# Six lots of query scores instead of four in the main bursts of an attention and cosine-FFN kernel

## The chip, the cores and the metric

One Trainium2 (trn2) chip, one core of it. The metric is device time in microseconds (us); less is better. The time before is 1098.57 us, the median of three runs (1098.48 to 1100.44).

## The reference, cut to what matters

```python
B, N, C = 4, 12480, 128            # 49 agents, float32
scale = 1.0 / np.sqrt(C)
def sm(a, b):                      # softmax of scale * a @ b.T
    s = scale * (a @ b.transpose(0, 2, 1))
    e = np.exp(s - s.max(-1, keepdims=True))
    return e / (e.sum(-1, keepdims=True) + 1e-09)
agent_v = sm(agents, k) @ v        # (4, 49, 128): keys and values of a batch give 49 rows
out = sm(q, agents) @ agent_v      # (4, 12480, 128): every query looks at 49 agents
h = out.reshape(-1, 128) @ w_in    # (49920, 2048)
result = (h * np.cos(h)) @ w_out   # (49920, 128)
```

## The kernel before

The agents' values are multiplied into the first weights, batch by batch, so that the weights of 49 agents for a query (`pT`) go straight into the FFN. The 49,920 queries are 52 groups of 960 (13 for each batch), each in two chunks of 480 columns, and the 2048 hidden units are 8 pairs of 128. **A step** is one pair for one chunk: 16 steps a group, 208 a batch, 832 in all. In step n PE multiplies into `ph` (L1063, two matmuls of 480 columns in one of three `ph` tiles), ScalarE takes the cosine (L1066), VectorE the product `(c - 1) * h` (L1072), and PE multiplies the product of four steps before into the output's accumulator (L1088). At a chunk's end two small matmuls (L1084, L1085) are added and ScalarE copies the accumulator out. That stream goes on from start to end, and everything else is worked into it.

**Lots.** For each group of queries, its scores with the agents must be ready before its first step: 64 small matmuls of 49 columns (`query_parts`, L169), a copy out of PSUM (L689), the maximum over the agents on VectorE (L693), a subtraction on GpSimd (L695), later an exponential, a sum, and the turning into `pT` (L785 to L796: PE, ScalarE, GpSimd). `query_both` does the scores of two groups in one `ph` tile, with one copy (L734) and one maximum (L736). A lot of keys of the next batch is alike, 64 small matmuls, a copy and a running maximum. A lot of values (`values`, L595) is 64 small matmuls with the exponentials of the keys (L516), whose result VectorE copies into `av` (L604, the first) or adds to it (L606). A small lot's result, and the output's accumulator too, is a tile `one`, of which there are two. A lot's queries are loaded from HBM by SP into `xt` (three tiles), its values into `vt` (six).

**When.** `plan` and `early_plan` hold what is to be emitted in which step; `early_plan` comes ahead of the products that are still owed, `plan` behind them. `extra` looks for the next free step whose place in the chunk allows a lot. `spread_out` and `mixed` spread the lots over the steps evenly. A load may not be issued before the loads that were emitted 24 steps earlier. SP issues its loads one after another, each when its tile is free.

**Bursts.** ScalarE's exponentials need another table than its cosine. So they are gathered: in step 97 of every batch's 208 (steps 97, 305, 513, the main bursts, and 721, the last) ScalarE does the exponential of seven groups of queries (L746), of all keys of the next batch (L587) and of six more groups, with a table load before and after (in the last, of five groups alone). For seven steps from there the order on PE, VectorE and ScalarE is the program's (`as_traced`), and the products of the burst's next steps are emitted only with the third step behind it. Here `fill` gives work to the other engines: one lot of queries at the burst's step, two at once (`query_both`) a step later, then one more lot and the first two lots of values, which need the key exponential. `judged` emits four reductions (L381) a step behind the burst and a small verdict (L393, L394) three steps behind it: they look at the folded weights of the batch before and serve a fallback. They are there in the bursts at 305, 513 and 721. The other eleven lots of values, and the lots of queries left of the first seven of the next batch (five in the last batch), are spread over the steps from the burst's + 5 on.

Of the kernel before, what the change touches and what calls it, by code (L numbers as in the profile page):

```python
# [9 lines left out]
F32 = mybir.dt.float32  # L10
# [8 lines left out]
P = 128  # L19
# [22 lines left out]
VT = 6  # L42
# [4 lines left out]
def agent_attention_cos_ffn(ctx, tc, qT, kT, v, vk, vk_rest, agT, w_in, w_out, outT):  # L47
    nc = tc.nc
    NB, _, N = qT.shape
# [5 lines left out]
    DFF = w_in.shape[0] * 512  # L55
# [83 lines left out]
    def load(dst, src):  # L139

        ins = nc.sync.dma_start(dst, src)
        traced = nc.cur_bb.bb.instructions[-1]
        if pinned[0]:
            tc.keep_in_program_order(ins)
        elif len(issued) > AHEAD:
            tc.add_manual_dep(traced, issued[-AHEAD].name, mybir.DependencyInfo(mybir.DependencyClass.NoSync,
                              mybir.DependencyReason.DATA), reason="held")
        latest[0] = traced
# [107 lines left out]
    class Agents:  # L256
# [58 lines left out]
        def value_tile(self, g):  # L315
            vt = self.sb.tile([TT, GT, P], F32, name="vt", bufs=VT)
            for h in range(2):
                load(vt[:, h * HT:(h + 1) * HT], v[self.b, g, h])
            return vt

        def values(self, g):
            vt = self.value_tile(g)
            po = self.psum()[:KR, :P]
            e = self.part(g).rearrange("p t a -> p (t a)")
            for t in range(HT):
                for h, width in enumerate((HI, NA)):
                    x = h * HT + t
                    mm = nc.tensor.matmul(po[h * HI:h * HI + width], e[:, x * NA:x * NA + width], vt[:, x, :],
                                          start=(t == 0), stop=(t == HT - 1))
                    if t == h == 0:  # L330
                        behind(mm)
            if g == 0:
                self.sums = self.sb.tile([KR, P], F32, name="sums", bufs=1)
                nc.vector.tensor_copy(self.sums, po)
            else:
                nc.vector.tensor_add(self.sums, self.sums, po)
# [198 lines left out]
    class Later(First):  # L535
# [53 lines left out]
        def add(self, g):  # L589
            s = self.s[:, 8 * g:min(8 * g + 8, NT_K)]  # L590
            es = self.es[:, :s.shape[1]]
            with kept_behind([nc.gpsimd.engine]):
                nc.gpsimd.tensor_add(es, self.s[:, :8] if g == 1 else es, s)

        def values(self, g):  # L595
            e = self.part(g)
            w, k, _ = e.shape
            vt = self.sb.tile([P, 2 * 4, P], F32, name="vt", bufs=VT)[:w, :k]
            load(vt, vk[self.b, g] if g + 1 < NL else vk_rest[self.b])
            po = self.psum()[:, :NA]  # L600
            self.weighted(po, [e[:, t] for t in range(k)], vt, True, True)
            if g == 0:
                self.clear()
                nc.vector.tensor_copy(self.av[:, :NA], po)  # L604
            else:
                nc.vector.tensor_add(self.av[:, :NA], self.av[:, :NA], po)  # L606
# [28 lines left out]
    with ExitStack() as pools:  # L635
# [40 lines left out]
        def query_parts(n, piece, wide=False, by_vector=False):  # L676
            b, g = n // NG, n % NG
            src = qT[b, :, g * GRP:(g + 1) * GRP]
            if wide:
                ps = scores_twice(sb.tile([P, 2 * 512], F32, name="xt", bufs=3)[:, :GRP], src, b, pair())  # L680
                yield
            else:
                ps = query_scores(sb, src, b, small()).rearrange("p (h t) a -> p h t a", h=2)
                yield
            if n == piece[0]:
                piece_tiles(piece)
            e = e_of[n].rearrange("p (h t) a -> p h t a", h=2)
            if not wide:
                (nc.vector.tensor_copy if by_vector else nc.scalar.copy)(e, ps)  # L689
                ps = e  # L690
            mx = sb.tile([QT, GT], F32, name="mx2")
            mx = mx.rearrange("p (h t) -> p h t", h=2)
            nc.vector.reduce_max(mx, ps, axis=AX.X)  # L693
            on = nc.vector if wide else nc.gpsimd
            on.tensor_sub(e, ps, mx.unsqueeze(3).to_broadcast([QT, 2, HT, NA]))  # L695
# [28 lines left out]
        def query_both(n, piece):  # L724

            ps = pair()
            for i in range(2):
                g = (n + i) % NG
                query_scores(sb, qT[n // NG if n % NG + i < NG else n // NG + 1, :, g * GRP:(g + 1) * GRP], (n + i) // NG, ps[:, i])
            if n == piece[0]:  # L730
                piece_tiles(piece)
            i = n - piece[0]
            e = e_of[piece][:, i * GT:(i + 2) * GT]
            nc.vector.tensor_copy(e.rearrange("p (i t) a -> p i (t a)", i=2), ps[:QT, :, :GT * NA])  # L734
            mx = sb.tile([QT, 2 * GT], F32, name="mx3")
            nc.vector.reduce_max(mx, e, axis=AX.X)  # L736
            for i in range(2):
                part = slice(i * GT, (i + 1) * GT)
                nc.gpsimd.tensor_sub(e[:, part], e[:, part], mx[:, part].unsqueeze(2).to_broadcast([QT, GT, NA]))

        def query(*args):
            for _ in query_parts(*args):
# [170 lines left out]
        def in_parts(f, *args):  # L913
            if f is query:
                yield from query_parts(*args)
            else:
                yield f(*args)
# [22 lines left out]
            return [(query, n, piece, *how) for n in piece]  # L940

        def judged(at):
            for x, part in later:
                for c in range(DFF // 512):
                    early_plan(at + 1, x.largest, c, part)
                early_plan(at + 3, x.judge)
            later.clear()

        def early_fill(at, todo):

# [7 lines left out]
                early_plan(n, next, x)  # L958
                (early_plan if n + 1 < at + 5 else plan)(n + 1, list, x)

        def fill(at, queries, values):

            taken.update(range(at, at + 5))
            for i, work in enumerate(('q', 'D', 'qvv', '', '')):
                on = early_plan if 0 < i < 4 else plan
                for x in work:
                    if x == "D" and len(queries) > 1:
                        on(at + i, query_both, *queries.pop(0)[1:3])
                        queries.pop(0)
                    else:  # L970
                        todo = dict(q=queries, D=queries, v=values)[x]
                        if todo:
                            on(at + i, list, in_parts(*todo.pop(0)))
                if 2 <= i < 4:
                    on(at + i, summed, at, 9)

        t = spread_out(scored(early), 0, 0) + 2
        t += (LAG + 1 - t) % NP
# [16 lines left out]
        for b in range(1, NB):  # L995
            o, ps = (b - 1) * PER, pieces[b - 1]
            at = o + BURST
            qs = [x for piece in ps for x in scored(piece)][ahead:]
            ks = [(ab[b].scores, g) for g in range(3 if b == 1 else 0, NG)]
            before = sum(1 for x in qs) - AFTER  # L1000
            t = spread_out(mixed(ks, qs[:before]), t, at - TURN, True)
            t = extra(t, ab[b].across, dense=True)
            plan(t - 1, ab[b].top)
            t = extra(t + 1, ab[b].spread, dense=True) + 1
            for g in range(NL):
                plan(t + g, ab[b].shift, g)
            t = spread_out(qs[before:], t, at - 5, True)
            assert t < at, (t, at)
            work = dict(A=(query_exp, ps[0]), B=(query_exp, ps[1]), K=(pinned_exp, ab[b]))
            burst(at, [work[x] for x in ('A', 'K', 'B')])  # L1010
            fresh = scored(pieces[b][0], False, True)
            ahead = len(fresh)
            vs = [(ab[b].values, g) for g in range(NG)]
            judged(at)
            fill(at, fresh, vs)
            fresh = [x[:3] for x in fresh]
            for g in range(1, NL):
                plan(at + 44 + 3 * g, ab[b].add, g)
            t, end = at + 5, o + PER - 26
            todo = mixed(vs, fresh)  # L1020
            for i, x in enumerate(todo):
                t = extra(t, *x, dense=True) + 1
                if i + 1 < len(todo):
                    t += max(0, (end - t) // (len(todo) - i - 1) - 1)
            t = extra(t, ab[b].folded) + 1
            t = extra(t, ab[b].inverse) + 1
            i = b % 2
            for c in range(DFF // 512):
                t = extra(t, ab[b].project, c, a[i], dense=True) + 1
            t = extra(t, ab[b].project_out, wio, b1[i], b2[i], dense=True)  # L1030
            later.append((ab[b], a[i]))
            t += 1
            assert t < o + PER + 4, (t, o + PER)
# [1 line left out]
        t = spread_out([x for piece in pieces[NB - 1] for x in scored(piece)][ahead:], t, at - 6)  # L1035
        assert t < at
        burst(at, [(query_exp, piece) for piece in pieces[NB - 1]])
        judged(at)
        fill(at, [], [])

        def pinned_largest(c):
            tc.keep_in_program_order(key.largest(c, a[0]))
# [247 lines left out]
```

## Time and profile before

| | |
|---|---|
| median of three runs | 1098.57 us |
| the profiled execution's own time | 1100.26 us |
| its span, first to last instruction | 1098.5 us |
| PE busy (matmul) | 1044.0 us, 95% |
| VectorE (DVE) busy | 1027.6 us, 94% |
| ScalarE (ACT) busy | 954.1 us, 87% |
| GpSimd (POOL) busy | 460.5 us, 42% |
| mean granted TensorE clock | 0.984 of full speed |

Busy shares are means over stages with different limits: between the bursts ScalarE is not the limit, in a burst it works without a break while PE and VectorE wait. [...]

### The profile page before, as it was taken

Reading aid. Unit: us, or ns where it says so; the run is one execution under the profiler, and the core shown is the slowest. Engines: PE = TensorE matmul, PEld = TensorE weight load, DVE = VectorE, ACT = ScalarE, POOL = GpSimd, SP = SyncE. Lnnn points to the kernel's source line nnn. Section 1 sums busy time; section 2 is a strip of 40 time slices with the busy share of each in tenths; the row PEclk is TensorE's granted clock in tenths of the full one; section 3 lists DMA queues with packets and bytes.
Section 4 is the critical chain, followed back from the end, with each engine's and each line's share of the span. In section 5 each row is a group of like instructions: output and inputs, shape, how many; then the busy total and the mean of one; then the engine's idle time right before and its main releaser. Section 6 shows DMA issues by size and latency. Waiting matters only on the chain.

```text
span 1098.5 us, 28945 instructions
## 1 busy us (share of the span) xinstructions
PE 1044.0 (95%) x12029; PEld 797.2 (73%) x12029; DVE 1027.6 (94%) x1139; ACT 954.1 (87%) x1196; POOL 460.5 (42%) x761
## 2 busy tenths in 40 slices
PE   6888999799999999989999999989999999989997
PEld 2766777687877787677786788767776777767775
DVE  6879999699999999989998999979998999999997
ACT  4678888898989999899888999888888999999996
POOL 2432326784522223786543131678362312252220
PEclk9899999899999999999999999989999999989999
DMA  9933566522002245442111234441100000000001
GB/s 357 339 92 115 150 188 226 168 83 90 23 36 95 77 131 175 137 157 79 44 54 58 93 95 164 140 151 58 60 20 37 18 36 19 37 18 36 19 37 40
DMA packets 32557, 108.49 MB, mean 99 GB/s; under 512 B 3616, under 2 KB 4896, under 8 KB 32416
## 3 DMA queue, kind: packets, MB, share of 16 engines
q1 hardware_dynamic: 32416, 106.55, 29.0%
q8 instruction: 97, 1.59, 0.6%
q14 instruction: 44, 0.36, 0.1%
HBM read 80.97 MB, written 25.56 MB: 97 GB/s over the span
## 4 chain that ended last, share of the span: by engine, by line
PE 52%; DVE 29%; ACT 7%; POOL 6%; issue 4%; DMA 1%; SPq 0%; ACTq 0%; POOLq 0%; DVEq 0%
DVE r L1072 26%; PE ph L1063 21%; PE one L1088 18%; ACT c L1066 4%; POOL s L584 3%; PE one L516 3%; PE one L169 2%; PE one L1084 1%; PE one L552 1%; PE one L1085 1%; PE one L785 1%; ACT s L587 1%; PE one L373 1%; DVE run L559 1%; ACT osb L1095 1%
## 5 line engine op out<-in xcount | busy, mean ns | idle before, releaser
L1072 DVE SCALAR_TENSOR_TENSOR r<-c,ph 128x960 fp32r<-128x960 f32 x832 | 909.4, 1147 | 31.3 <-ACT c L1066 29.3
L1066 ACT ACTIVATE c<-ph 128x960 f32<-128x960 f32 x832 | 790.2, 979 | 99.4 <-PE ph L1063 75.7
L1063 PE MATMUL ph<-pT,a 113*128 113x480 f32 x1664 | 537.2, 403 | 18.2 <-DVE r L1072 11.8
L1088 PE MATMUL one<-r,w 128*128 128x480 f32 x1664 | 503.6, 389 | 0.4 <-DVE r L1072 0.4
L1063 PEld LDWEIGHTS ph<-pT,a 113*128 113x128 f32 x1664 | 287.7, 190 | 141.3 <-DVE r L1072 76.2
L1088 PEld LDWEIGHTS one<-r,w 128*128 128x128 f32 x1664 | 309.1, 190 | 50.8 <-DVE r L1072 1.4
L771 POOL TENSOR_TENSOR p<-e,rz 126x392 f32<-126x392 f32 (+1 forms) x52 | 44.2, 851 | 314.1 <-PE one L785 300.3
L796 POOL TENSOR_TENSOR pT<-p,pT 49x480 fp32r<-49x480 f32 x104 | 126.9, 1220 | 7.9
L795 POOL CAST pT<-p 49x480 fp32r<-49x480 f32 x104 | 60.7, 584 | 61.9 <-ACT p L790 57.5
L695 POOL TENSOR_TENSOR e<-e,mx 126x392 f32<-126x392 f32 x43 | 36.2, 842 | 90.4 <-DVE mx L693 90.0
L757 POOL TENSOR_TENSOR tree<-tree 126x96 f32<-126x96 f32 (+1 forms) x141 | 43.8, 311 | 10.6
L1095 ACT COPY osb<-one 128x480 f32<-128x480 f32 x80 | 44.5, 556 | 3.9 <-PE one L1088 3.9
L516 PEld LDWEIGHTS one<-s,vt 128*32 128x32 f32 (+1 forms) x2352 | 31.1, 115 | 22.6 <-issue 13.7
L516 PE MATMUL one<-s,vt 128*32 128x49 f32 (+1 forms) x2352 | 37.3, 216 | 10.2 <-ACT s L587 7.0
L169 PEld LDWEIGHTS one<-ag,xt 128*32 128x32 f32 (+1 forms) x2752 | 32.9, 109 | 17.4 <-issue 14.4
L169 PE MATMUL one<-ag,xt 128*32 128x49 f32 (+1 forms) x2752 | 39.1, 209 | 2.9 <-issue 2.9
L584 POOL TENSOR_TENSOR s<-s,mxb 128x392 f32<-128x392 f32 (+1 forms) x39 | 34.3, 911 | 17.1 <-DVE mxb L580 17.1
L1084 PE MATMUL one<-pT,b 113*128 113x480 f32 x104 | 40.5, 389 | 0.0
L1085 PE MATMUL one<-pT,b 113*128 113x480 f32 x104 | 40.0, 385 | 0.0
L552 PEld LDWEIGHTS one<-ag,xt 128*32 128x32 f32 x2340 | 28.3, 110 | 15.1 <-issue 7.7
L552 PE MATMUL one<-ag,xt 128*32 128x49 f32 x2340 | 33.6, 209 | 2.0 <-DVE s L556 2.0
L757 POOL TENSOR_TENSOR tree<-e 126x192 f32<-126x192 f32 (+1 forms) x47 | 28.9, 615 | 11.2 <-ACT e L746 8.9
(151 smaller groups left out, 654.9 us busy)
## 6 DMA issues: line engine op xcount, KB each, us to landing
xt<-qT SPq DMA_DIRECT2D x51, 480.0 KB, 4.0
outT<-osb SPq DMA_DIRECT2D x51, 480.0 KB, 2.7
xt<-kT SPq DMA_DIRECT2D x42, 512.0 KB, 3.8
vt<-vk SPq DMA_DIRECT2D x36, 512.0 KB, 4.5
c<-kT SPq DMA_DIRECT2D x6, 512.0 KB, 6.1
c<-vk SPq DMA_DIRECT2D x6, 512.0 KB, 7.4
xt<-vk SPq DMA_DIRECT2D x6, 512.0 KB, 7.6
vt<-w_in SPq DMA_DIRECT2D x8, 256.0 KB, 6.4
```

Of the source, the lines that this page charges most:

```text
L169: mm = nc.tensor.matmul(out[at:at + n], xt[:, t * TT + lo:t * TT + lo + n], ag, start=True, stop=True)
L516: mm = nc.tensor.matmul(po[rows], vt[:, x, rows], e, start=(first and x == 0), stop=(last and x + 1 == len(es)))
L552: mm = nc.tensor.matmul(ps[j * QS:(j + 1) * QS, t], xt[:, t * w + j * QS:t * w + (j + 1) * QS], ag[:, self.b, :], start=True, stop=True)
L584: nc.gpsimd.tensor_sub(s, s, self.mxb.unsqueeze(1).to_broadcast(list(s.shape)))
L757: nc.gpsimd.tensor_add(t[:, :, :w], src[:, :, :w], src[:, :, w:2 * w])
L795: nc.gpsimd.tensor_copy(pT[own, c], p[own])
L796: nc.gpsimd.tensor_sub(pT[other, c], p[own], pT[own, c].bitcast(F32))
L1063: nc.tensor.matmul(ph[:, j, :CH], ai[:, f], pTs[q % 3][:, c], start=True, stop=True)
L1066: nc.scalar.activation(cos, h, AF.Sin, bias=HALF_PI, scale=1.0)
L1072: nc.vector.scalar_tensor_tensor(r, cos, 1.0, h, op0=ALU.subtract, op1=ALU.mult)
L1088: nc.tensor.matmul(po, w1[:, f, :], r[:, j, :], start=(f == 0), stop=(f == NF - 1))
L1095: nc.scalar.copy(osb[:, c * CH:(c + 1) * CH], po)
```

## The change

A main burst takes six lots of queries instead of four where the batch has them (the last has five): one, a pair, and three more. The lots are generators with more places to stop (`yield`), so that their parts can be put in another order: at the burst's step the whole of the first lot, a step later the scores and the copies of the pair and of the fourth, then scores, copies and maxima of the rest. VectorE's copies stand ahead of its maxima there. The loads of the first two lots of values are emitted at the burst's step, with the values themselves staying two steps behind it. The four reductions are emitted two steps behind the burst instead of one, behind the lots of queries and ahead of the values; in the last burst as well. The lots left over start nine steps behind the burst instead of five.

```diff
@@ -592,11 +592,21 @@
             with kept_behind([nc.gpsimd.engine]):
                 nc.gpsimd.tensor_add(es, self.s[:, :8] if g == 1 else es, s)
 
+        vt = {}
+
+        def value_tile(self, g):
+            w, k = (P, 8) if g + 1 < NL else (REST, 2)
+            vt = self.sb.tile([P, 2 * 4, P], F32, name="vt", bufs=VT)[:w, :k]
+            load(vt, vk[self.b, g] if g + 1 < NL else vk_rest[self.b])
+            return vt
+
+        def value_loads(self, *gs):
+            self.vt = {g: self.value_tile(g) for g in gs}
+
         def values(self, g):
             e = self.part(g)
             w, k, _ = e.shape
-            vt = self.sb.tile([P, 2 * 4, P], F32, name="vt", bufs=VT)[:w, :k]
-            load(vt, vk[self.b, g] if g + 1 < NL else vk_rest[self.b])
+            vt = self.vt.pop(g) if g in self.vt else self.value_tile(g)
             po = self.psum()[:, :NA]
             self.weighted(po, [e[:, t] for t in range(k)], vt, True, True)
             if g == 0:
@@ -688,6 +698,7 @@
             if not wide:
                 (nc.vector.tensor_copy if by_vector else nc.scalar.copy)(e, ps)
                 ps = e
+                yield
             mx = sb.tile([QT, GT], F32, name="mx2")
             mx = mx.rearrange("p (h t) -> p h t", h=2)
             nc.vector.reduce_max(mx, ps, axis=AX.X)
@@ -731,12 +742,16 @@
                 piece_tiles(piece)
             i = n - piece[0]
             e = e_of[piece][:, i * GT:(i + 2) * GT]
+            yield
             nc.vector.tensor_copy(e.rearrange("p (i t) a -> p i (t a)", i=2), ps[:QT, :, :GT * NA])
+            yield
             mx = sb.tile([QT, 2 * GT], F32, name="mx3")
             nc.vector.reduce_max(mx, e, axis=AX.X)
             for i in range(2):
                 part = slice(i * GT, (i + 1) * GT)
                 nc.gpsimd.tensor_sub(e[:, part], e[:, part], mx[:, part].unsqueeze(2).to_broadcast([QT, GT, NA]))
+
+            yield
 
         def query(*args):
             for _ in query_parts(*args):
@@ -940,11 +955,12 @@
             return [(query, n, piece, *how) for n in piece]
 
         def judged(at):
+            checks = []
             for x, part in later:
-                for c in range(DFF // 512):
-                    early_plan(at + 1, x.largest, c, part)
+                checks += [(x.largest, c, part) for c in range(DFF // 512)]
                 early_plan(at + 3, x.judge)
             later.clear()
+            return checks
 
         def early_fill(at, todo):
 
@@ -958,21 +974,27 @@
                 early_plan(n, next, x)
                 (early_plan if n + 1 < at + 5 else plan)(n + 1, list, x)
 
-        def fill(at, queries, values):
+        def fill(at, queries, values, checks):
 
             taken.update(range(at, at + 5))
-            for i, work in enumerate(('q', 'D', 'qvv', '', '')):
-                on = early_plan if 0 < i < 4 else plan
-                for x in work:
-                    if x == "D" and len(queries) > 1:
-                        on(at + i, query_both, *queries.pop(0)[1:3])
-                        queries.pop(0)
-                    else:
-                        todo = dict(q=queries, D=queries, v=values)[x]
-                        if todo:
-                            on(at + i, list, in_parts(*todo.pop(0)))
-                if 2 <= i < 4:
-                    on(at + i, summed, at, 9)
+            if queries:
+                f, g = values[0][0], values[0][1]
+                plan(at, f.__self__.value_loads, g, g + 1)
+                lots = [query_parts(*queries.pop(0)[1:]), query_both(*queries.pop(0)[1:3])]
+                queries.pop(0)
+                lots += [query_parts(*queries.pop(0)[1:]) for _ in range(min(3, len(queries)))]
+                for k in range(3):
+                    plan(at, next, lots[0], None)
+                for i, order in ((1, (1, 2, 1, 2)), (2, (3, 1, 3, 4, 2, 3, 4, 4))):
+                    for x in order:
+                        if x < len(lots):
+                            early_plan(at + i, next, lots[x], None)
+            for x in checks:
+                early_plan(at + 2, *x)
+            for _ in range(2 if values else 0):
+                early_plan(at + 2, *values.pop(0))
+            for i in (2, 3):
+                early_plan(at + i, summed, at, 9)
 
         t = spread_out(scored(early), 0, 0) + 2
         t += (LAG + 1 - t) % NP
@@ -1011,12 +1033,11 @@
             fresh = scored(pieces[b][0], False, True)
             ahead = len(fresh)
             vs = [(ab[b].values, g) for g in range(NG)]
-            judged(at)
-            fill(at, fresh, vs)
+            fill(at, fresh, vs, judged(at))
             fresh = [x[:3] for x in fresh]
             for g in range(1, NL):
                 plan(at + 44 + 3 * g, ab[b].add, g)
-            t, end = at + 5, o + PER - 26
+            t, end = at + 9, o + PER - 26
             todo = mixed(vs, fresh)
             for i, x in enumerate(todo):
                 t = extra(t, *x, dense=True) + 1
@@ -1035,8 +1056,7 @@
         t = spread_out([x for piece in pieces[NB - 1] for x in scored(piece)][ahead:], t, at - 6)
         assert t < at
         burst(at, [(query_exp, piece) for piece in pieces[NB - 1]])
-        judged(at)
-        fill(at, [], [])
+        fill(at, [], [], judged(at))
 
         def pinned_largest(c):
             tc.keep_in_program_order(key.largest(c, a[0]))
```

## Rows read from the trace of the kernel before

**Rows 1.** The page's chain that ended last, by engine; q is an engine's queue.

```profile
PE 52%; DVE 29%; ACT 7%; POOL 6%; issue 4%; DMA 1%; SPq 0%; ACTq 0%; POOLq 0%; DVEq 0%
```

**Rows 2.** Windows, products L1072 alone: six steps from each main burst's product.

```profile
200.69:220.63 19.94, 6.81 (x7) 0.83 0.68 218
461.30:479.28 17.98, 6.70 (x8) 0.91 0.70 219
720.01:739.44 19.43, 6.83 (x8) 0.82 0.55 171
```

**Rows 3.** Windows over stretches of half clock, all engines; PEclk is third from last.

```profile
209.61:216.43 6.82, 5.56 (x74) 4.62 (x75) 2.33 (x3) 5.41 (x6) 6.11 (x16) 0.50 0.77 242
469.02:472.43 3.41, 2.81 (x109) 2.42 (x113) 0.21 (x1) 3.38 (x3) 2.72 (x10) 0.50 0.17 22
```

**Rows 4.** Windows, L1072 alone: 85 steps, second and third main burst.

```profile
489.52:591.09 101.57, 93.45 (x86) 1.00 0.17 57
749.70:849.23 99.53, 93.08 (x87) 1.00 0.13 48
```

**Rows 5.** The same windows: L693, a lot of queries each, then L606, values.

```profile
489.52:591.09 101.57, 1.10 (x2) 1.00 0.17 57
749.70:849.23 99.53, 0.00 (x0) 1.00 0.13 48
...
489.52:591.09 101.57, 1.99 (x10) 1.00 0.17 57
749.70:849.23 99.53, 1.97 (x10) 1.00 0.13 48
```

**Rows 6.** Timeline of ScalarE in the second main burst (start, us, instructions).

```profile
472.33 1.84 ACT L1066 ACTIVATE c<-ph 128x960 f32<-128x960 f32 x2
```

**Rows 7.** Timeline of VectorE in the second main burst; idle time in brackets.

```profile
463.51 2.45 DVE L381 TENSOR_REDUCE big<-a 113x1 f32<-113x512 f32 x4
...
467.76 0.56 DVE L689 COPY e<-one 126x392 f32<-126x392 f32 x1
...
471.26 0.21 DVE L604 COPY av<-one 128x49 f32<-128x49 f32 x1 [2.27 <-PE one L516]
...
473.34 1.15 DVE L1072 SCALAR_TENSOR_TENSOR r<-c,ph 128x960 fp32r<-128x960 f32 x1
```

**Rows 8.** Timeline of PE: second main burst, then stalls in first and third.

```profile
464.71 0.90 PE L169 MATMUL one<-ag,xt 128*32 128x49 f32 x64
469.02 1.03 PE L516 MATMUL one<-s,vt 128*32 128x49 f32 x35 [3.41 <-ACT s L587]
...
471.52 1.31 PE L516 MATMUL one<-s,vt 128*32 128x49 f32 x64 [0.31 <-DVE av L604]
...
205.46 0.64 PE L169 MATMUL one<-ag,xt 128*30 128x49 f32 x41 [1.17 <-issue]
...
726.04 0.38 PE L169 MATMUL one<-ag,xt 128*32 128x49 f32 x16 [1.77 <-issue]
```

**Rows 9.** Timeline of VectorE behind the second burst: waiting, a lone maximum.

```profile
479.28 7.60 DVE L1072 SCALAR_TENSOR_TENSOR r<-c,ph 128x960 fp32r<-128x960 f32 x7 [0.36 <-ACT c L1066]
...
486.79 0.55 DVE L693 TENSOR_REDUCE mx<-e 126x8 f32<-126x392 f32 x1
```

**Rows 10.** Line L141, two loads of queries in the second burst, with landing.

```profile
L141 SPq DMA_DIRECT2D xt<-qT x1: 328/328/328, 462.6 to 462.6; - x1
...
DMA to landing us min/median/max: 4.7/4.7/4.7
...
L141 SPq DMA_DIRECT2D xt<-qT x1: 328/328/328, 463.8 to 463.8; - x1
...
DMA to landing us min/median/max: 6.8/6.8/6.8
```

**Rows 11.** Timeline of GpSimd: a lot's subtraction, and the making of pT.

```profile
463.67 0.84 POOL L695 TENSOR_TENSOR e<-e,mx 126x392 f32<-126x392 f32 x1 [3.03 <-DVE mx L693]
...
486.29 2.51 POOL L796 TENSOR_TENSOR pT<-p,pT 49x480 fp32r<-49x480 f32 x2
```

## The prediction

> **What bounds the kernel now.** I began with the chain of waits: 52% of it is PE and 29% VectorE, so the two share the bound [rows 1]. Which of them it is depends on the stage, so I read stretches next. Between bursts one step is one product of L1072 on VectorE, and the windows over 85 steps (a burst's step + 15 to + 100) give 101.57 us after the second main burst and 99.53 after the third, the first like the second [rows 4]. Both stretches hold ten lots of values; the second has two lots of queries, the third none [rows 5]. So two lots of queries among the steps cost 2.04 us, 1.0 each, more than the 0.55 of its maximum on VectorE [rows 9].
>
> In a burst ScalarE bounds. In the second it is with exponentials and tables until its first cosine at 472.33 [rows 6]. VectorE has the lots and four reductions (2.45) to do, and waits 2.27 us before the first copy into av; PE waits 3.41 us for the key exponential before the first values [rows 7, 8]. That idle time is where two more lots would go. But the burst does not end with ScalarE alone: the product that follows the cosine of 472.33 starts on VectorE at 473.34, just behind the two sums of values, and the second values end on PE at 471.52 + 1.31 = 472.83 [rows 7, 8]. Anything that makes these values later makes the burst longer, with no slack to speak of.
>
> Last, six steps from a burst's product on take 19.94, 17.98 and 19.43 us [rows 2]. [...] The differences to the second burst, 1.96 and 1.45 us, are my price of a clock that is still low when the steps resume.
>
> **The change, part by part.**
>
> *Lots out of the steps.* Batches 1 and 2 move two lots into the burst, batch 3 one, as it has only five. Among the steps, a burst's step + 12 now holds values instead of a lot of queries: 0.55 against 0.20 on VectorE, so at least 0.35 and at most the mean of 1.0 [rows 5, 9]. For a lone lot, with one step's work around it, I take 0.5. In the 85 steps one lot of queries stays (it comes eight steps later than the first did) and one goes. By the mean that is 1.0; the one that stays lies where lots are wide apart and should cost the 0.5 of a lone one, which leaves 1.5. I take 1.5 + 0.5 for batches 1 and 2 and 0.5 for batch 3: -4.5 us (bounds -3.0 and -5.5).
>
> *The third values later.* They stood five steps behind the burst, with 0.20 on VectorE and then 0.36 us of waiting [rows 5, 9], as PE was behind. At + 12 they take the place counted above. Per burst -0.4, together -1.2 (bounds 0 and -1.7).
>
> *Six lots in the burst.* PE's order becomes: first lot; pair and fourth lot; fifth; sixth; two values. All single lots and both values share one PSUM slot, the output's accumulator holding the other, so each waits for the copy before it. Step by step for the second burst. The sixth lot's queries can be loaded only when the pair has been scored: issued at 463.76, landed 6.8 us later, 470.56; the fifth's 4.7 us after 462.63 [rows 10]. Between them a load of values was issued, which is now emitted eight steps later and held behind a later lot. I take 469.2 for the sixth (bounds 467.3, when the fifth landed, and 470.6). Scores 0.9, a copy 0.6: 470.7 [rows 7, 8]. The first values run to 471.7. VectorE meanwhile owes the last maximum (0.55), then the four reductions (2.45), which now stand behind the lots, and only then the copy into av: 470.7 + 0.55 + 2.45 + 0.2 = 473.9. The second values wait for that copy and end at 475.0 instead of 472.8: +2.2. Queued behind on VectorE are the products; on PE the next step's matmuls. In the first burst nothing is judged (-2.45), but two more lots of small matmuls meet PE's stalls with nothing released, such as 1.17 and 1.77 us ("issue", [rows 8]), two at about 1: +1.7. In the third, five lots, with the reductions and one stall: +1.7. Together +5.6 (bounds 0, if all is done when the exponential is, and +9, if queries land as late as now and every lot stalls).
>
> [...]
>
> *The clock.* PE's longest wait in the burst, 3.41 us, is filled with lots, and what is left are waits of up to 2 us around the last copies. If the clock is full when the steps resume, the first and third bursts gain 1.96 + 1.45 = 3.4; if it falls as before, 0. The second burst, low for one short stretch only, is the nearest row. I take three quarters, -2.6.
>
> *GpSimd.* Two more subtractions of 0.84 stand ahead of the next pT's making, whose first half is done in the middle of the 2.51 us that start at 486.29 [rows 11]. The step that needs it follows closely, so its matmuls may come up to 1.7 us later; no row shows how much of that is spare, and I take 1.3, near the upper end, as nothing on GpSimd is idle between. The terms above put them 2.2 - 0.4 - 0.5 = 1.3 later: no cost, but a floor under any gain in the second burst. The cover is the longer burst itself.
>
> *Moved at no cost:* the value loads at the burst's step (the first values waited for the exponential, not for a load [rows 8]), the reductions in the last burst (VectorE waits there for the exponential in any case), the added yields, which emit nothing.
>
> Sum: -4.5 - 1.2 + 5.6 - 2.6 = -2.7 us. The profiled execution took 1100.26 us with a span of 1098.5; the median of three is 1098.57, 1.69 lower, so I set the difference against the median: 1095.9. A difference under about 0.2%, 2.2 us, cannot be told from none here.
>
> **Rivals.**
>
> *Hidden altogether.* The queries land early and the lots end before the key exponential; then the +5.6 is gone but for the floor of GpSimd (about 2 in the second burst, where the sum would fall below it). That gives -8.3 + 2 = -6.3: 1092.3. For it: VectorE's 2.27 and PE's 3.41 us of idle time. Against: loads of 4.7 and 6.8 us. Chance 0.15.
>
> *Late queries take it all back.* With the landing at 470.56 as now, the first two bursts are longer by 1.4 more each, +8.4: sum 0.1, 1098.7. It decides from a landing about 1 us later than I assume. For it: three loads in flight already slow each other, 4.7 then 6.8 [rows 10]. Against: the load of values between them goes. Chance 0.22.
>
> *The clock falls in the burst and stays low.* The lots leave PE waiting in many short pieces; if the granted clock is 0.50 from the last lots to well into the steps in all three bursts, the -2.6 is gone, the second burst loses about 1.7 as the others did, and lots and values at half clock cost some 0.4 each (1.31 against 0.9 us for 64 matmuls), 0.8 a burst: -4.5 - 1.2 + 5.6 + 1.7 + 2.4 = +4.0, 1102.6. It ends on the slow side once low stretches reach over 3.4 us in every burst. For it: two of three fell so before; against: PE's longest wait is halved. Chance 0.17. [...]
>
> **How the numbers follow.** The forecast has 0.46, with a range of its own from 1094.2 to 1097.4 (the clock term at its two ends, a little of the burst term); some two thirds of that, 0.30, lies below 1096.4, where faster begins, and 0.16 is within 0.2%. Faster: 0.30 + 0.15 = 0.45. Same: 0.16 + 0.22 = 0.38. Slower: 0.17. The range goes from 1092.8, in the middle of the hidden case, to 1101.0, which leaves out most of the low-clock case.
>
> **What would show it.** Right: six steps from the bursts' products of about 19, 19.8 and 19 us; the copy into av behind four reductions; the second values at the burst's end about 2 us later; 100.0 us over the 85 steps of batches 1 and 2, 99.5 for batch 3. Wrong: PE still idle for 3 us before the first values (hidden), a fifth or sixth lot that waits for its queries beyond 470 in the second burst's terms, or a granted clock of 0.50 past the burst in all three.

## The result and the profile after

The changed kernel takes 1115.71 us (median of four runs, 1111.10 to 1119.17) against 1099.30 of the kernel before in the same comparison: the ratio is 1.0138, 95% interval 1.0115 to 1.016. It is slower by some 15 us, where 1095.9 was forecast and the range ended at 1101.0.

The profiled execution is the quickest of the four, 1111.10 us with a span of 1109.3; what follows explains its 10.8 us over the span before. The median is 4.6 us longer still, and no trace shows where. Windows over the products (L1092 in this kernel), six steps from each main burst's product, as in [rows 2]; columns are window, length, VectorE's busy time in these products, granted clock, DMA share, GB/s:

```profile
200.50:225.16 24.66, 6.56 (x7) 0.72 0.62 209
464.55:491.52 26.97, 6.55 (x8) 0.75 0.58 190
730.94:750.63 19.69, 6.55 (x7) 0.91 0.57 184
```

and over the 85 steps that follow nine steps later, as in [rows 4], here for all three bursts:

```profile
235.23:335.63 100.40, 93.24 (x86) 1.00 0.18 63
501.59:602.02 100.43, 93.22 (x86) 1.00 0.18 63
760.71:860.11 99.40, 93.13 (x87) 1.00 0.13 48
```

The loss is in two places: the first burst has 24.66 us instead of 19.94, the second 26.97 instead of 17.98, together 13.7. The third, with five lots, stands at 19.69 against 19.43, so the three bursts took 14.0 us more. The steps between gained, 101.57 to 100.43 behind the second burst, but that is only 1.1 us a batch.

The second burst on VectorE, from the fifth lot's copy on; idle time and what ended it in brackets, as in [rows 7]:

```profile
473.85 0.57 DVE L699 COPY e<-one 126x392 f32<-126x392 f32 x1 [3.62 <-PE one L169]
474.33 1.02 DVE L704 TENSOR_REDUCE mx<-e 126x8 f32<-126x392 f32 x2
476.07 0.57 DVE L699 COPY e<-one 126x392 f32<-126x392 f32 x1 [0.72 <-PE one L169]
480.46 0.56 DVE L704 TENSOR_REDUCE mx<-e 126x8 f32<-126x392 f32 x1 [3.82 <-POOL e L706]
480.93 2.45 DVE L381 TENSOR_REDUCE big<-a 113x1 f32<-113x512 f32 x4
483.31 0.20 DVE L614 COPY av<-one 128x49 f32<-128x49 f32 x1
485.16 0.21 DVE L616 TENSOR_TENSOR av<-av,one 128x49 f32<-128x49 f32 x1 [1.66 <-PE one L516]
```

Here is a wait that the kernel before had nowhere: 3.82 us for GpSimd, between the sixth lot's copy and its maximum. The maximum goes into a tile `mx2`, of which there are two. The lots that come alone (first, fourth, fifth, sixth) take them in turn, and a tile is free when GpSimd has subtracted that maximum. The sixth needs the fourth's tile. GpSimd's timeline at that time shows where that subtraction is:

```profile
475.27 1.64 POOL L752 TENSOR_TENSOR e<-e,mx 126x392 f32<-126x392 f32 x2
...
477.32 0.60 POOL L772 TENSOR_TENSOR tree<-e 126x192 f32<-126x192 f32 x1
...
479.58 0.84 POOL L706 TENSOR_TENSOR e<-e,mx 126x392 f32<-126x392 f32 x1
```

It stands in GpSimd's queue behind the pair's two subtractions (1.64) and a whole tree sum, and ends at 480.42; VectorE goes on at 480.46. In the third burst the fifth lot is the last single one and needs the first lot's tile, free long before. The view of line L704 over the whole run has this wait twice, 6.9 us in all (3.12 in the first burst):

```profile
its engine sat idle before it (us, times) until:
  POOL e L706: 6.9, 2
```

PE in the same burst, as in [rows 8]:

```profile
466.85 0.46 PE L169 MATMUL ph<-ag,xt 128*32 128x49 f32 x23 [0.58 <-issue]
467.83 0.90 PE L169 MATMUL one<-ag,xt 128*32 128x49 f32 x64 [0.52 <-DMA xt<-qT]
468.66 0.71 PE L1108 MATMUL one<-r,w 128*128 128x480 f32 x2
469.20 0.60 PE L1083 MATMUL ph<-pT,a 113*128 113x480 f32 x2
470.19 0.63 PE L169 MATMUL one<-ag,xt 128*32 128x49 f32 x36 [0.39 <-DMA xt<-qT]
472.94 0.86 PE L169 MATMUL one<-ag,xt 128*32 128x49 f32 x28 [2.12 <-issue]
474.47 1.53 PE L169 MATMUL one<-ag,xt 128*32 128x49 f32 x64 [0.67 <-DVE e L699]
476.74 1.00 PE L516 MATMUL one<-s,vt 128*32 128x49 f32 x35 [0.74 <-ACT c L1086]
479.04 0.87 PE L516 MATMUL one<-s,vt 128*32 128x49 f32 x29 [1.30 <-issue]
483.56 1.53 PE L516 MATMUL one<-s,vt 128*32 128x49 f32 x64 [3.65 <-DVE av L614]
```

The last row is the end of VectorE's wait: the second values stand still for 3.65 us for the copy into av. But PE is late before that too. "Issue" takes 0.58, 2.12 and 1.30 us, two lots wait for their queries, and 64 matmuls take 1.53 us instead of 0.90. That last is the clock; windows over the two low stretches, as in [rows 3] (PE, its weight loads, VectorE, ScalarE, GpSimd, clock, DMA share, GB/s):

```profile
206.57:220.22 13.65, 8.92 (x263) 7.26 (x262) 5.27 (x11) 6.72 (x5) 12.00 (x34) 0.50 0.60 201
472.81:486.46 13.65, 7.16 (x224) 6.10 (x225) 6.38 (x14) 4.56 (x4) 12.13 (x33) 0.50 0.44 147
```

13.65 us at 0.50 in each of the first two bursts, against 6.82 and 3.41 before. In the second it begins in PE's wait of 2.12 us.

### The profile page after: what moved, and what is told of

Its sections match the earlier page's. It is cut to its first block, busy times and chain, and to the rows that moved or that the text cites. A ratio compares the mean times of both kernels' runs of the same rounds, so it can differ in the third digit from the quotient of the medians.

```text
span 1109.3 us, 28938 instructions
## 1 busy us (share of the span) xinstructions
PE 1045.6 (94%) x12029; PEld 799.9 (72%) x12029; DVE 1029.9 (93%) x1144; ACT 952.9 (86%) x1191; POOL 460.8 (42%) x761
## 4 chain that ended last, share of the span: by engine, by line
PE 50%; DVE 30%; POOL 7%; ACT 6%; issue 4%; DMA 1%; SPq 0%; ACTq 0%; POOLq 0%; DVEq 0%
DVE r L1092 27%; PE ph L1083 21%; PE one L1108 18%; ACT c L1086 4%; POOL s L584 3%; PE one L516 2%; POOL tree L772 2%; PE one L1104 2%; PE one L552 1%; PE one L1105 1%; PE one L800 1%; PE one L169 1%; ACT e L761 1%; PE one L373 1%; DVE run L559 1%
## 5 line engine op out<-in xcount | busy, mean ns | idle before, releaser
L1092 DVE SCALAR_TENSOR_TENSOR r<-c,ph 128x960 fp32r<-128x960 f32 x832 | 909.1, 1149 | 28.5 <-ACT c L1086 26.8
L169 PEld LDWEIGHTS one<-ag,xt 128*32 128x32 f32 (+1 forms) x2752 | 35.4, 114 | 23.8 <-issue 17.6
L169 PE MATMUL one<-ag,xt 128*32 128x49 f32 (+1 forms) x2752 | 42.0, 215 | 9.7 <-issue 5.8
L516 PEld LDWEIGHTS one<-s,vt 128*32 128x32 f32 (+1 forms) x2352 | 31.8, 117 | 23.9 <-issue 11.8
L772 POOL TENSOR_TENSOR tree<-tree 126x96 f32<-126x96 f32 (+1 forms) x141 | 44.1, 312 | 10.6
L584 POOL TENSOR_TENSOR s<-s,mxb 128x392 f32<-128x392 f32 (+1 forms) x39 | 34.4, 918 | 17.1 <-DVE mxb L580 17.1
L772 POOL TENSOR_TENSOR tree<-e 126x192 f32<-126x192 f32 (+1 forms) x47 | 28.8, 612 | 11.8 <-ACT e L761 8.9
```

Of the source, the lines that this page charges most:

```text
L169: mm = nc.tensor.matmul(out[at:at + n], xt[:, t * TT + lo:t * TT + lo + n], ag, start=True, stop=True)
L516: mm = nc.tensor.matmul(po[rows], vt[:, x, rows], e, start=(first and x == 0), stop=(last and x + 1 == len(es)))
L584: nc.gpsimd.tensor_sub(s, s, self.mxb.unsqueeze(1).to_broadcast(list(s.shape)))
L772: nc.gpsimd.tensor_add(t[:, :, :w], src[:, :, :w], src[:, :, w:2 * w])
L1092: nc.vector.scalar_tensor_tensor(r, cos, 1.0, h, op0=ALU.subtract, op1=ALU.mult)
```

## The experiments

The ratio is always that to the kernel before, run beside it, with its 95% interval. That kernel's median went from 1099.30 to 1101.57 us between the comparisons, so what one run takes more or less than another is the difference of their ratios here, in us of 1100. The theory at the start: VectorE waits for a tile of the maximum. The rivals: too much work for PE in the burst (its instructions, late queries, a low clock), and the four reductions that now stand ahead of the copy into av.

**Four tiles for the maximum**, in both places where `mx2` is made (the other is that of the keys); the first of them:

```diff
-            mx = sb.tile([QT, GT], F32, name="mx2")
+            mx = sb.tile([QT, GT], F32, name="mx2", bufs=4)
```

> The changed kernel with four tiles instead of two for the maximum of a single lot (mx2); the instructions and their order on every engine stay the same, only the wait for a free tile goes. Theory: in the first two main bursts the fourth single lot's maximum waits 3.1 and 3.8 us for GpSimd to finish with an earlier maximum behind its tree sums, and the copy into av and the second values queue behind it. Then VectorE's waits on GpSimd vanish, the second values end about 2.0 us earlier in the first burst and 3.5 in the second, nothing changes in the third: about -5.5 us, some 1110 at the median against 1115.7. Rival (too much work in the burst: PE's stalls, late queries, low clock): within 1.5 us of 1115.7. Rival (the four reductions ahead of the values): the same, within 1.5 us.

1112.35 us, 1.0113 (1.0087 to 1.0138). The line's view has no wait for GpSimd any more, only this:

```profile
its engine sat idle before it (us, times) until:
  ACT e L699: 0.8, 2
```

So the wait is what I took it for, but the time fell by 2.8 us, half of what was expected, with intervals that overlap: its price was open, and at least 9 us were something else. In the one profile the six steps take 26.09, 24.14 and 22.38 us: the second burst is shorter than in the changed kernel, the first and third are longer, and the third had no such wait to lose. A single profile of a burst is no more exact than that. In the second burst of this kernel PE still shows

```profile
474.66 0.54 PE L169 MATMUL one<-ag,xt 128*32 128x49 f32 x28 [1.84 <-issue]
...
477.98 1.00 PE L516 MATMUL one<-s,vt 128*32 128x49 f32 x35 [0.72 <-issue]
480.87 0.87 PE L516 MATMUL one<-s,vt 128*32 128x49 f32 x29 [1.89 <-issue]
```

**The reductions ahead of the lots again.**

```diff
             taken.update(range(at, at + 5))
+            for x in checks:
+                early_plan(at + 1, *x)
...
-            for x in checks:
-                early_plan(at + 2, *x)
```

> The changed kernel with the four reductions (L381) back at the burst's step + 1, ahead of the pair's copy; all else as changed. Rival (the reductions between the lots and the values make the burst long): 2.4 us less in the second and third burst each, about -5, some 1111. Theory (the tile of the maximum): the wait for GpSimd stays where it is in the second burst, the copy into av comes 2.4 earlier after it, and the third burst gains about 1.0: -3 to -3.5, some 1112.5, and VectorE still waits over 3 us on GpSimd in the first two bursts.

1114.31 us, 1.013 (1.0105 to 1.0154): no difference from the changed kernel that can be told. VectorE's wait for GpSimd grew to 13.8 us in its trace. The reductions alone, which should have given back 5 us, are not the cause. The edit also changed GpSimd's order, so the longer wait is not theirs alone.

**Five lots.**

```diff
-                lots += [... for _ in range(min(3, len(queries)))]
+                lots += [... for _ in range(min(2, len(queries)))]
```

> The changed kernel with five lots in every main burst (one, a pair, two more) instead of six; the sixth is spread among the steps. Theory and the rival of too much work both expect the first two bursts to come out like the third now (+0.3 us against before), with one lot of queries out of the steps for each: about -1 in all against the kernel before, some 1098 to 1100. If PE's stalls and not the sixth lot's tile are the cause, a good part of the loss stays: over 1104.

1107.99 us, 1.0066 (1.0043 to 1.0089). No lot waits for a tile of the maximum here, yet 7 us are lost, with six steps of 21.85, 21.40 and 20.42 us behind the bursts' products. The expectation of 1098 to 1100 fell, and with it the theory as the whole cause. That the third burst of the changed kernel, with the same five lots, had 19.69 us, nearly level with before, was probably a good draw: it has 22.38 with four tiles and 20.42 here.

**Four tiles and the reductions where VectorE waited.** The edit of four tiles above, and:

```diff
-                for i, order in ((1, (1, 2, 1, 2)), (2, (3, 1, 3, 4, 2, 3, 4, 4))):
+                for i, order in ((1, (1, 2, 1, 2)), (2, (3, 1)), (2, (3, 4, 2, 3, 4, 4))):
...
+                    if order == (3, 1):
+                        for x in checks:
+                            early_plan(at + 2, *x)
```

> Four tiles for the maximum as in the first experiment, and the four reductions put behind the pair's maximum, where VectorE waited 3.6 us for the fifth lot's scores in the second burst. Theory: -5.5 of the first experiment and 2.4 more in the second burst, about 1 in the third, so some 1106 to 1107. The rival of too much work: 1112 to 1114, the reductions' share alone.

1108.53 us, 1.0077 (1.0054 to 1.01). Against four tiles alone 4.0 us less, about what was expected of the reductions, with intervals that just overlap.

**A quarter of the matmuls in the last three lots.**

```diff
+        if few:
+            for t in range(0, GT, HT):
+                beside(xt, t, ag[:, b, :].unsqueeze(1).to_broadcast([P, HT, NA]), ps[:, t:t + HT])
+            return ps
```

> The first experiment's kernel (four tiles for the maximum), with each of the fourth, fifth and sixth lots in a main burst scored by 16 matmuls of 196 columns instead of 64 of 49: the same columns through PE, 144 matmuls and as many weight loads less. These lots score a quarter of their queries, four times over, so their part of the output is not the reference's. Theory (PE waits for its own instructions, the idle time marked issue): those waits in the lots go, one or two of 1 to 2 us a burst, and the clock has less reason to fall; 2 to 4 us less a burst, some 1102 to 1106 against 1112.4. Rival (late queries, or the chain of copies through one PSUM slot): within 2 us of 1112.4.

1105.52 us, 1.0044 (1.0028 to 1.006): 7.6 us less than four tiles alone, with the same columns through PE. PE's idle time marked issue falls from 11.4 us in the three bursts' six steps to 5.0, while its waits for a transfer grow from 1.5 to 6.4: the loads come into the place of the stalls. So the count of instructions, weight loads included, has a price, paid in stalls or through the clock that goes with them.

**No loads for the last three lots.**

```diff
+        if box:
+            xt = box[0]
+        else:
             xt = sb.tile([P, 2 * 512], F32, name="xt", bufs=3)[:, :GRP]
             load(xt, src)
+            if box is not None:
+                box.append(xt)
```

> The first experiment's kernel, with the fourth to sixth lots of a main burst reading the first lot's queries again instead of loading their own, so that their part of the output is not the reference's; the matmuls stay. Rival (late queries, and the transfers in a burst): PE's waits for a transfer (0.3 to 0.5 us) and the stalls that come with them go; 3 to 5 us less in all, some 1107 to 1109. Theory (count of instructions): only the short waits for a transfer go, -1 to -2, some 1111, and the idle time marked issue stays at 2 us or more a burst.

1104.69 us, 1.004 (1.0023 to 1.0057): 8.0 us less than four tiles alone. I had expected 1 to 2 from the short waits for a transfer that the trace names; the rival, late queries and transfers, was right in the time and even too low. But it also expected the stalls to go, and the idle time marked issue stays at 11.8 us. The waits for a transfer that are gone were 1.5 us in all, so how the loads cost the rest is not shown.

**Both at once.** The two diffs above together.

> The two edits of the fifth and sixth experiments at once: the fourth to sixth lots of a main burst have 16 matmuls of 196 columns each and read the first lot's queries instead of loading their own (so their part of the output is not the reference's); four tiles for the maximum. If PE's instructions and the lots' queries are two separate prices, 7.5 us each of the 12 that are left, both go: 1096 to 1099, at or below the kernel before. If they are one (both only make PE start the lots and values sooner, with the rest set by the chain of copies through one PSUM slot or by the clock), about 1104 again.

1099.70 us, 0.9994 (0.9981 to 1.0007). That is just above the 1096 to 1099 expected of two prices. They nearly add: 13.1 us off the kernel with four tiles, against 7.6 + 8.0 = 15.6. Its six steps, in windows as above:

```profile
203.83:221.22 17.39, 6.54 (x7) 0.90 0.52 176
462.84:480.31 17.47, 6.48 (x8) 1.00 0.45 151
721.93:739.70 17.77, 6.56 (x7) 0.90 0.26 89
```

These bursts hide six lots from PE and VectorE, 4.7 us shorter together than before (19.94, 17.98 and 19.43) and hardly at a low clock. Even so the whole is level with the kernel before. Most of the gain is lost in the nine steps behind the six, here in the kernel before and then in this one:

```profile
220.63:230.88 10.25, 9.73 (x10) 1.00 0.25 79
479.28:489.53 10.25, 9.73 (x10) 1.00 0.35 119
739.44:749.70 10.26, 9.73 (x9) 1.00 0.08 31
...
221.22:233.22 12.00, 9.95 (x10) 1.00 0.17 46
480.31:492.27 11.96, 9.95 (x11) 1.00 0.15 45
739.70:750.67 10.97, 9.97 (x10) 1.00 0.18 50
```

They take 4.2 us more. In each of the three PE waits for `pT`, which GpSimd makes: 1.96, 1.92 and 0.94 us, where the kernel before has no such wait. This is the second:

```profile
490.52 0.70 PE L1093 MATMUL ph<-pT,a 113*128 113x480 f32 x2 [1.92 <-POOL pT L820]
```

GpSimd's timeline has no wait from 466.47 to there, with the lots' subtractions and the sums ahead of that `pT`. Hidden from PE and VectorE, the lots are not hidden from GpSimd.

**Two tiles for the maximum again, in that kernel.**

```diff
-            mx = sb.tile([QT, GT], F32, name="mx2", bufs=4)
+            mx = sb.tile([QT, GT], F32, name="mx2")
```

> The kernel with few matmuls and no loads for the fourth to sixth lots, with two tiles for the maximum again; the order on every engine is that of the kernel with four, and the same part of the output is not the reference's. Theory (the fourth single lot's maximum waits for a tile that GpSimd frees behind its sums): in the first two bursts the wait is now the last to end, 3 us or more each, 5 to 8 us in all, some 1105 to 1108 against 1099.7; the third burst as before. Rival (the wait only fills time in which PE is behind anyway): within 2 us of 1099.7.

1107.76 us, 1.0056 (1.0042 to 1.007), with the same order on every engine: 6.8 us for the two tiles alone. The line's view names the wait:

```profile
its engine sat idle before it (us, times) until:
  POOL e L715: 12.0, 2
```

The rival, that the wait only fills time in which PE is behind, falls where PE is not behind. In the changed kernel PE is behind, and there the same two tiles were worth 2.8 us, not clear of noise.

**Four lots in the new order.**

```diff
-                lots += [... for _ in range(min(3, len(queries)))]
+                lots += [... for _ in range(min(1, len(queries)))]
```

> The changed kernel with four lots in a main burst as before (one, a pair, one), in the changed order: copies ahead of maxima, reductions behind the lots, value loads first, the third values later. Theory (the loss is the fifth and sixth lot's): the kernel before within 2 us, 1098 to 1102. Rival (the order does it): 1104 or more.

1102.93 us, 1.0019 (1.0006 to 1.0032). The changed order costs some 2 us; the rest is the fifth and sixth lot's.

**The third values later, alone.**

```diff
-            t, end = at + 5, o + PER - 26
+            t, end = at + 9, o + PER - 26
```

> The kernel before with nothing changed but the lots that are left over starting nine steps behind the burst instead of five. Predicted by the document's own term: -0.4 us for each main burst, about -1.2 in all. In the trace of the changed kernel the ten steps behind a burst's first six gained only 0.2 each; by that, within 1 us of the kernel before.

1101.70 us, 1.0005 (0.9994 to 1.0016). No gain that can be told, and the forecast's 1.2 us lies outside the interval.

**Five tiles for queries**, and five for values to make room, with six lots, four tiles for the maximum and the reductions behind the pair's maximum.

```diff
-VT = 6
+VT = 5
...
-        xt = sb.tile([P, 2 * 512], F32, name="xt", bufs=3)[:, :GRP]
+        xt = sb.tile([P, 2 * 512], F32, name="xt", bufs=5)[:, :GRP]
```

> Six lots, four tiles for the maximum, the four reductions behind the pair's maximum, and five tiles for queries (xt) instead of three, with five for values (vt) instead of six to make room: the fourth and fifth lots' queries can be loaded before the burst. The whole result is computed. Theory (late queries are about 7.5 us of what is left, the reductions 3): 1100 to 1103, against 1108.5 with three tiles. If only the transfers' being there matters and not when they come, 1106 to 1109.

1104.15 us, 1.0038 (1.0024 to 1.0052): 4.3 less than with three tiles, a little short of what was expected. The sixth lot's queries are still loaded only behind the first lot, at 463.12 in the second burst, but PE waits for no transfer in the three bursts. Its idle time marked issue is 10.6 us there.

**Five lots with five tiles for queries.** The edits of the run before on tiles and reductions, two tiles for the maximum, and:

```diff
-                lots += [... for _ in range(min(3, len(queries)))]
+                lots += [... for _ in range(min(2, len(queries)))]
```

> Five lots in each main burst, the reductions behind the pair's maximum, five tiles for queries and five for values. All queries of the burst can be loaded before it. Theory: of the 7 us that five lots lost, the late queries' part and the reductions' go: 1099 to 1102. Otherwise 1105 to 1108 as with three tiles.

1101.86 us, 1.0022 (1.001 to 1.0034): 4.8 less than five lots with three tiles and the reductions behind.

**The kernel before with five tiles for queries.** The two edits on tiles alone:

```diff
-VT = 6
+VT = 5
...
-        xt = sb.tile([P, 2 * 512], F32, name="xt", bufs=3)[:, :GRP]
+        xt = sb.tile([P, 2 * 512], F32, name="xt", bufs=5)[:, :GRP]
```

> The kernel before with five tiles for queries and five for values, nothing else: what the tiles are worth by themselves. In its bursts no wait for queries was in the trace, so within 1.5 us of the kernel before; a gain of 2 us or more would say that the tiles and not the lots carry the two experiments beside it.

1100.79 us, 1.0004 (0.9995 to 1.0013): the tiles by themselves are worth nothing that can be told. Loading ahead gained 4.3 and 4.8 us here where six or five lots stood in a burst, and with four nothing that can be told.

**Two tiles for the maximum again, with six lots and five tiles for queries.**

```diff
-            mx = sb.tile([QT, GT], F32, name="mx2", bufs=4)
+            mx = sb.tile([QT, GT], F32, name="mx2")
```

> Six lots, the reductions behind the pair's maximum, five tiles for queries and values, with two tiles for the maximum again; the same order on every engine as with four. Theory: 4 to 7 us more than the 1104.15 with four, some 1108 to 1111. Rival: within 2 us of it.

1117.08 us, 1.0142 (1.0127 to 1.0158): 11.4 us more than with four tiles for the maximum, beyond the 4 to 7 expected. The trace tells why: with the reductions moved, GpSimd's order is another, and the fourth lot's subtraction comes behind still more sums, so that VectorE waits 7.19 us for it, and 3.02 in the first burst. VectorE, then GpSimd:

```profile
487.43 0.56 DVE L704 TENSOR_REDUCE mx<-e 126x8 f32<-126x392 f32 x1 [7.19 <-POOL e L706]
...
486.55 0.84 POOL L706 TENSOR_TENSOR e<-e,mx 126x392 f32<-126x392 f32 x1
```

No version that computes the whole result was quicker than the kernel before. With six lots hidden from PE and VectorE the time is 0.9994 of it, and GpSimd's queue is what PE waits for then, 1.96, 1.92 and 0.94 us. No run put the lots' subtractions ahead of the sums on GpSimd.

## Why the prediction was wrong, point by point

- **What bounds the burst: right.** It said that the burst ends with the second values on PE and the sums on VectorE, and that what makes them later makes the burst longer without slack. That is what happened.
- **The step that failed: the six lots in the burst, +5.6.** With the clock's -2.6 the forecast has 3.0 us for the three bursts; their six steps took 14.0 more. The term counted the PSUM slot, the tiles for queries and VectorE's order, and missed that a lot's maximum also holds one of two tiles until GpSimd has used it. [rows 11] showed the subtractions on GpSimd, and I asked only whether they delay the next `pT`, not who waits for them. Putting the two tiles back costs 6.8 us where nothing else on PE is late; in the changed kernel itself, taking them away gives 2.8. No rival had this wait; the slow one that I gave 0.17 rested on the clock.
- **The same term, its other parts: the larger share.** PE's stalls marked issue and late queries were in it, with one or two stalls of 1 us a burst and a delay of the queries; its upper bound, +9, was too low as well. With four tiles, so without the wait, the kernel is 1.0113, some 12 us above before; taking instructions out gives 7.6 back, taking loads out 8.0, both 13.1. Taking fewer lots agrees: 1.0066 with five, 1.0019 with four. The rival of late queries had the right direction, with a price of 2.8 us.
- **The clock, -2.6: wrong sign.** I argued that lots fill PE's longest wait. They broke it into several, the low clock lasted 13.65 us in two bursts, and in all three it reached 0.9 to 1.4 us past the first product behind the burst, which was one of the signs of being wrong. Half clock costs 0.63 us for each 64 matmuls (1.53 against 0.90; the prediction's 0.4 came from a row that was only partly at half clock), so at most 2.5 a burst for the fifth and sixth lots and two lots of values. In the experiments it goes along with the time: 0.50 for 34.1 us in the three bursts with four tiles, 23.9 with few matmuls, 17.1 without loads, 6.8 with both, against 17.1 in the kernel before. No run changed the clock alone: how much of the prices above goes through it stays open.
- **Lots out of the steps, -4.5: mis-sized.** The 85 steps gained 1.1 us in each of the first two batches (100.40 after 101.49, and 100.43 after 101.57, where 100.0 was forecast), and the nine ahead of them 0.2 a burst instead of 0.5: some 2.9 in all.
- **GpSimd, a floor: right, and too low.** It put the next `pT` up to 1.7 us later and called this a floor under any gain in the second burst. In the changed kernel the longer bursts covered it. Where they did not, with few matmuls and no loads, PE waited 1.96, 1.92 and 0.94 us. So the rival of lots hidden altogether, -6.3 with 2 for this floor, has its nearest run at -0.7.
- **The third values later, -1.2: nothing**, by the run that changed it alone.
- **The stalls marked issue.** From the stall of 0.58 to that of 2.12 us PE did 23 + 64 + 2 + 2 + 36 = 127 matmuls, from there to that of 1.30 again 28 + 64 + 35 = 127, with 127 weight loads each, 254 instructions; with the two waits for a semaphore that the trace has in each stretch, 256. All eight stalls marked issue in the three bursts of the changed kernel lie a multiple of 256 instructions apart, to within one. Each ends 1.2 to 1.5 us behind a packet of 16,384 bytes on the profile's queue q8, of the kind instruction; that of 2.12 us ends at 472.94, and its packet stands in the window from 470.4 to 471.6:

```profile
q8 instruction: 1, 0.02, 5.3%
```

The three of the second burst took 0.58, 2.12 and 1.30 us, and the kernel with four tiles took 7.6 us less with 144 matmuls and weight loads fewer in each of the first two bursts and 96 in the third. That PE waits for such a packet itself is an inference from these counts and times, and no run moved the stalls alone.

## What to carry to other kernels

Before work is moved into another engine's shadow, list every tile that the moved work holds, small ones too, with who frees it and what stands in that engine's queue ahead of that instruction: here two tiles of 32 bytes a partition made VectorE wait 3.12 and 3.82 us for GpSimd's sums. Count the instructions and the transfers that idle time is filled with, not their busy time alone; the fifth and sixth lots were small in busy time (at full clock 0.90 us of PE for the matmuls of one, 0.57 and 0.56 of VectorE), and most of the price came with the instructions and the loads of the lots from the fourth on (7.6 and 8.0 us, 13.1 for both), with a low clock beside them (0.50 for 13.65 us in each of two bursts). And see first what the moved work costs where it is, and which other engine handles it: the steps gained some 2.9 us, and where the lots were hidden from PE and VectorE, GpSimd took 4.2 us back behind the bursts.

## What the runs showed of the hardware that was not expected

In the changed kernel's three bursts, where matmuls of 49 columns stand densely, PE's stalls marked issue lie 256 instructions apart within a burst (127 matmuls, 127 weight loads and two semaphore waits; once 255, with one wait). They take 0.3 to 2.1 us each, and PE goes on 1.2 to 1.5 us behind the end of a packet on the instruction queue q8. With 196 columns a matmul instead of 49 in the lots from the fourth on, for the same columns, this idle time fell from 11.4 to 5.0 us in the three bursts. And the lots in PE's long wait did not bring the full clock: 0.50 was granted for 13.65 us in each of the first two bursts, where the kernel before had 6.82 and 3.41. Before it fell PE had idled twice in the first burst, 1.18 and 1.15 us, and in the second it was in its wait of 2.12 us.
